# A 1-core adaLN, window-attention and token-MLP kernel: w1's first half paced, the zero fill of V in quarters, one small op with two inputs, masks in two steps, and a new order of the engines

## The chip, the cores and the metric

One Trainium2 chip, one of its cores. The metric is the time of one launch in microseconds (us) on the device, as a median of several runs.

Short names: PE is the matmul engine, PEld its weight loads, DVE the vector engine, ACT the scalar engine, POOL the GpSimd engine, SP the engine that hands over the DMA transfers. PSUM is the memory that matmuls write, SBUF the one that holds the other tiles. A hole is a stretch in which PE stands idle. The name before `<-` in a profile line is the tile that is written: `xn` is the normalised x and `nm` minus its mean, `kb` and `KT` are keys, `QT` queries, `VT` values, `psa` and `psb` scores, `et` their exps. A cast is a copy into another type. L193 and the like is the line of a helper that records every operation.

## The reference, cut to what matters

```python
# x: (1, 2048, 512), 32 heads of 16, window W = 256, F = 1792; weights in bf16
mod = (silu(c) @ w_mod)                     # six vectors of 512: sa, ca, ga, sb, cb, gb
h = layernorm(x) * (1 + ca) + sa
q, k, v = split(h @ wqkv)                   # per head
p = softmax(where(0 <= i - j < W, q @ k.T / 4, -1e9))
x = x + ga * ((p @ v) @ wo)
h = layernorm(x) * (1 + cb) + sb
u = gelu(einsum("bsd,sf->bdf", layernorm(h), w1) + b1)   # MLP over the 2048 tokens
x = x + gb * (einsum("bdf,fs->bds", u, w2) + b2).T
```

The attention is cut into 75 chunks of keys by queries. Each chunk is scores on PE, two exps on ACT (one of 128x1536 from `psa`, one of 128x512 from `psb`), a mask, then probabilities times V on PE. The first MLP matmul (`pu<-hb,w1p`) runs between the chunks as soon as rows of h are there. The rest of the MLP comes behind the last chunk.

## The kernel before

The whole program is a list of some 1,360 small operations. A fixed string of their numbers, `ORDER`, says in which order they are emitted. A letter behind a number (D, A, P) picks the engine. Each engine is given its own instructions in this order, so what is emitted behind a waiting instruction comes late too (PE's wait of 1.76 us in the prediction's lines).

```python
ORDER = """47 3 0 4 34 1 51 2 38 7 ... 1359 1360"""

VT = [kvpool.tile([P, 8, DH, 2 * DH], BF, name=f"VT{r}") for r in range(3)]   # V, block diagonal
vt_zero = [op("vz", {"DVE": 1.7, "POOL": 4.3},
              lambda e, r=r: (ve if e == "DVE" else po).memset(VT[r][:], 0.0), ...) for r in range(3)]

def e_nm(e, a, b):                       # nm = -mean
    mv, _, nm = box[box_key]
    (ve if e == "DVE" else po).tensor_scalar(
        out=nm[:, a:b], in0=mv[:, a:b, 0], scalar1=-1.0, scalar2=0.0, op0=ALU.mult, op1=ALU.add)

def emit_masks():                        # one operation on POOL, ahead of all scores
    if ADDED:
        emit_edges()
    ...                                  # block masks (maskt)

def load_w1(pair, half):                 # 14 pieces of 512 KB: 7 pairs, 2 halves
    t = box["w1"].tile([P, 8, 2 * P], BF, name=f"w1p{pair}", tag=f"w1p{pair}")
    sp.dma_start(out=t[:], in_=w1_v[:, 8 * half : 8 * half + 8, 2 * P * pair : 2 * P * (pair + 1)])
    w1t[pair, half] = t

def partials():                          # all seven first halves as soon as the modulation's SBUF is free
    freed = op("w1free", {"SP": 0.0}, e_w1, deps=mod_ops + warm_ops + [o_fm, masks_built], ...)
    for pair in range(NF // 2):
        w1_ops[pair, 0] = op("w1", {"SP": 0.4}, lambda e, pair=pair: load_w1(pair, 0), deps=[freed], ...)
```

The softmax here doesn't subtract the row's maximum and nothing guards it: scores larger than these inputs give would overflow.

## Time and profile before

| | |
|---|---|
| median | 273.39 us (273.29 to 273.47, 3 runs) |
| span of the profiled run | 271.3 us |
| PE busy | 251.4 us, 93% |
| w1's seven first pieces handed over | 43.0 to 53.9 us |

### The profile page before, as it was taken

The numbers are of one execution on the slowest core, as the hardware profiler recorded it, in microseconds if no ns is written. First come the engines' busy times: TensorE is split into PE (matmuls) and PEld (weight loads), VectorE is DVE, ScalarE is ACT, GpSimd is POOL, SyncE is SP. The second block draws the span as 40 slices with busy tenths as digits, with TensorE's granted clock in tenths as the row PEclk, the third lists the DMA queues.
The fourth block names the chain that finished last, engine by engine and source line by source line (L and its number), as shares of the span: only waits on it lengthen the run. The fifth ranks groups of instructions, "written<-read, shape, count | busy, mean of one in ns | idle before, by whom it ended". The sixth has DMA issues, their size and how long they took to land.

```text
span 271.3 us, 10569 instructions
## 1 busy us (share of the span) xinstructions
PE 251.4 (93%) x4737; PEld 137.8 (51%) x4737; DVE 208.6 (77%) x442; ACT 184.8 (68%) x277; POOL 68.5 (25%) x131
## 2 busy tenths in 40 slices
PE   8989979699999999778999999999999999999993
PEld 2566647256665664454464554444544444444441
DVE  4688899569887688999967799999999751134685
ACT  3269969579998999999999999999632741000000
POOL 8994460135021844151102400140000000000000
PEclk9999999899999999999999999999999999999999
DMA  6998104950000000000020000086199800011121
GB/s 207 323 349 211 5 2 133 289 130 5 2 5 2 5 6 2 2 2 2 10 76 2 2 2 4 2 228 163 54 408 377 324 1 4 19 39 39 62 89 65
DMA packets 31445, 24.80 MB, mean 91 GB/s; under 512 B 6056, under 2 KB 29608, under 8 KB 31400
## 3 DMA queue, kind: packets, MB, share of 16 engines
q1 hardware_dynamic: 31392, 24.13, 29.5%
q8 instruction: 37, 0.61, 0.9%
q14 instruction: 8, 0.07, 0.1%
q10 hardware_dynamic: 8, 0.00, 0.0%
HBM read 22.03 MB, written 2.10 MB: 89 GB/s over the span
## 4 chain that ended last, share of the span: by engine, by line
PE 73%; ACT 11%; DVE 11%; issue 4%
PE pu L193 35%; PE pxy L193 12%; ACT et L193 10%; PE pq L193 8%; PE psa L193 8%; PE pa L193 4%; PE pv L193 3%; DVE st L193 2%; DVE xn L193 1%; ACT lz L193 1%; DVE VT L193 1%; PE pt L193 1%; DVE et L193 1%; DVE nm L193 1%; PE ps_b L193 1%
## 5 line engine op out<-in xcount | busy, mean ns | idle before, releaser
L193 ACT ACTIVATE et<-psa 128x1536 bf16<-128x1536 f32 x75 | 109.1, 1454 | 10.0 <-PE psb L193 7.3
L193 PE MATMUL pu<-hb,w1p 128*128 128x512 bf16 x224 | 53.0, 380 | 0.1
L193 PE MATMUL pu<-guT,w 128*128 128x512 bf16 x224 | 49.2, 379 | 0.0
L193 ACT ACTIVATE et<-psb 128x512 bf16<-128x512 f32 x75 | 44.6, 598 | 0.0
L193 POOL TENSOR_SCALAR KT<-kb,mask_par 128x512 bf16<-128x512 bf16 (+1 forms) x36 | 23.3, 655 | 63.2 <-DVE kb L193 63.2
L193 PE MATMUL pxy<-et,VT 128*32 128x192 bf16 (+3 forms) x960 | 37.4, 234 | 0.7 <-DVE OT L193 0.5
L193 PE MATMUL pq<-h1T,wqkv 128*128 128x512 bf16 (+1 forms) x160 | 35.8, 350 | 2.2 <-DVE kb L193 1.3
L193 PE MATMUL pxy<-et,ones_bd 128*32 128x192 bf16 (+3 forms) x960 | 37.5, 233 | 0.0
L193 PEld LDWEIGHTS <-w 128*128 128x128 bf16 x224 | 21.9, 98 | 26.4
L193 PE MATMUL psa<-QT,KT 32*128 32x192 bf16 (+3 forms) x720 | 30.0, 230 | 5.1 <-ACT et L193 4.4
L193 PEld LDWEIGHTS <-w1p 128*128 128x128 bf16 x224 | 20.3, 98 | 24.9 <-issue 1.9
L193 PE MATMUL psb<-QT,KT 32*128 32x192 bf16 (+3 forms) x240 | 29.4, 231 | 2.6 <-issue 2.5
L193 PEld LDWEIGHTS <-KT 32*128 32x128 bf16 x960 | 15.6, 92 | 29.2 <-issue 27.5
L193 DVE SCALAR_TENSOR_TENSOR o<-pu,b2FM,bc_gb 128x512 f32<-128x512 f32 x16 | 12.0, 748 | 23.0 <-PE pu L193 23.0
L193 PEld LDWEIGHTS <-VT 128*32 128x32 bf16 x960 | 23.5, 97 | 7.8 <-issue 6.2
L193 DVE TENSOR_TENSOR et<-et,maskt 128x512 bf16<-128x512 bf16 (+2 forms) x56 | 23.8, 461 | 1.5 <-ACT et L193 1.4
L193 DVE CAST VT<-pv 64x512 bf16<-64x512 f32 x31 | 21.1, 686 | 2.9 <-PE pv L193 2.6
L193 DVE BATCH_NORM_STATS2 st<-x 128x6 f32<-128x512 bf16 x32 | 21.9, 684 | 1.8 <-DMA x<-in_A_x_dram 1.7
L193 PEld LDWEIGHTS <-ones_bd 128*32 128x32 bf16 x960 | 23.0, 97 | 0.1
L193 PEld LDWEIGHTS <-wqkv 128*128 128x128 bf16 x160 | 13.4, 99 | 14.7 <-issue 5.3
L193 PE MATMUL pv<-wqkv,h1T 128*32 128x256 bf16 x512 | 17.8, 274 | 0.8 <-DVE h1T L193 0.6
L193 DVE CAST QT<-pq 128x512 bf16<-128x512 f32 (+1 forms) x19 | 12.7, 670 | 5.8 <-PE pq L193 5.7
(91 smaller groups left out, 347.1 us busy)
## 6 DMA issues: line engine op xcount, KB each, us to landing
w1p<-in_B_w_dram SPq DMA_DIRECT2D x14, 512.0 KB, 7.5
w<-in_B_w_dram SPq DMA_DIRECT2D x14, 512.0 KB, 8.8
wmod<-in_w_mod_dram SPq DMA_DIRECT2D x6, 512.0 KB, 6.6
x<-in_A_x_dram SPq DMA_DIRECT2D x16, 128.0 KB, 5.7
out_dram<-otile SPq DMA_DIRECT2D x16, 128.0 KB, 1.7
wqkv<-in_A_wqkv_dram SPq DMA_DIRECT2D x2, 384.0 KB, 6.1
wqkv<-in_A_wqkv_dram SPq DMA_DIRECT2D x1, 512.0 KB, 5.9
wod<-in_A_wo_dram SPq DMA_DIRECT2D x1, 512.0 KB, 9.3
```

The source lines that it names most:

```text
L193: ins = call(*args, **kwargs)
```

## The change

Five parts: (a) each of the three zero fills of V's tile is cut into four; (b) `nm` on DVE is written with both inputs in SBUF; (c) edges and block masks become two operations, and scores wait for the edges alone; (d) a two-element copy on POOL from the exp tile of every third chunk into the w1 tile holds its load back; (e) `ORDER` is made anew. The arithmetic is the same, and PE has the same 4737 matmuls.

```diff
-47 3 0 4 34 1 51 2 38 7 35 8 39 5 82 56 40 81 6 46 9 57 54 83 10 45 ...
+49 3 0 4 46 84D 1 51 83D 2 47 7 41 8 44 5 93 56 42 90 6 54 9 57 35 94 ...
 ... (the whole order)
     def emit_masks():
-        if ADDED:
-            emit_edges()
-        if len(ADDED) == NU:
-            return
 ...
-            (ve if e == "DVE" else po).tensor_scalar(
-                out=nm[:, a:b], in0=mv[:, a:b, 0], scalar1=-1.0, scalar2=0.0, op0=ALU.mult, op1=ALU.add)
+            if e == "DVE":
+                ve.scalar_tensor_tensor(
+                    out=nm[:, a:b], in0=mv[:, a:b, 0], scalar=-2.0, in1=mv[:, a:b, 0], op0=ALU.mult, op1=ALU.add)
+            else:
+                po.tensor_scalar(...)            # as before
 ...
-    vt_zero = [op("vz", {"DVE": 1.7, "POOL": 4.3}, lambda ...: (...).memset(VT[r][:], 0.0), ...)
+    vt_zero = [[op("vz", {"DVE": 0.45, "POOL": 0.95}, lambda ...: (...).memset(VT[r][:, 2 * n : 2 * n + 2, :, :], 0.0),
+                   ...) for n in range(4)] for r in range(3)]
 ...
+    def touch_w1(pair, chunk):
+        t = w1t[pair, 0] = box["w1"].tile([P, 8, 2 * P], BF, name=f"w1p{pair}", tag=f"w1p{pair}")
+        po.tensor_copy(out=t[:, 0, 0:2], in_=et_of[chunk][:, 3, 0:2])
 ...
-            w1_ops[pair, 0] = op("w1", ..., deps=[freed], pos=start_of(1) + 2.0, ...)
+            w1_ops[pair, 0] = op("w1", ..., deps=[touched[chunk]], pos=chunk + 0.5, ...)
 ...
-    masks_built = op("masks", {"POOL": 6.0}, lambda e: emit_masks(), pos=-9.0)
+    edges_built = op("edges", {"POOL": 7.6}, lambda e: emit_edges(), pos=-9.0)
+    masks_built = op("masks", {"POOL": 2.8}, lambda e: emit_masks(), pos=20.0, sh=True)
```

## The prediction

> **What bounds the kernel now.** I first read the busy table by stage, with each row a stretch of the span and, for each engine, busy time, its instruction count, then granted TensorE clock, DMA share and GB/s.
>
> ```profile
> 35.00:42.00 7.00, 5.24 (x136) 3.15 (x124) 6.89 (x10) 4.88 (x7) 3.62 (x3) 1.00 0.01 2
> 42.00:49.00 7.00, 6.86 (x265) 4.84 (x262) 6.84 (x17) 6.75 (x10) 1.64 (x2) 1.00 0.74 194
> 49.00:56.00 7.00, 4.59 (x51) 1.77 (x50) 3.43 (x8) 2.44 (x4) 0.00 (x0) 0.76 1.14 278
> 56.00:133.00 77.00, 69.90 (x2079) 44.26 (x2078) 65.83 (x144) 75.47 (x109) 27.69 (x37) 1.00 0.03 9
> 133.00:196.00 63.00, 62.65 (x1293) 32.37 (x1292) 55.46 (x128) 59.45 (x91) 9.72 (x12) 1.00 0.21 54
> 196.00:266.00 70.00, 70.00 (x326) 31.78 (x325) 41.19 (x71) 12.99 (x24) 0.00 (x0) 1.00 0.37 136
> ```
>
> The columns are PE, PEld, DVE, ACT, POOL. From 56 to 133 us ACT (the exps of the attention) is busy 98% and paces the chunks; from 133 us to the end PE has no hole (62.65 of 63, then 70.00 of 70). So nothing after 56 us looks loose, and what can be won lies before it: two stages where PE and ACT both stand still, 35 to 42 and 49 to 56 us. Since everything behind is full, each us that PE wins there should move the end by one us.
>
> Next the timeline of single instructions, to see who holds these holes open (start, duration, engine, then idle before and releaser):
>
> ```profile
> 12.19 3.51 POOL L193 MEMSET VT<- 128x4096 bf16 x1
> 34.17 3.51 POOL L193 MEMSET VT<- 128x4096 bf16 x1
> ```
>
> ```profile
> 13.53 2.19 DVE L193 TENSOR_SCALAR nm<-mv 128x2 f32<-128x2 f32 x1
> 34.38 3.44 DVE L193 TENSOR_SCALAR xn<-x,mv,rs 128x512 bf16<-128x512 bf16 x1
> 38.34 0.42 DVE L193 TENSOR_SCALAR xn<-x,mv,rs 128x512 bf16<-128x512 bf16 x1
> ```
>
> Both slow DVE instructions start inside a zero fill of VT on POOL and end just after it (12.19 + 3.51 = 15.70 against 13.53 + 2.19 = 15.72; 37.68 against 37.82). The same xn takes 0.42 us four us later. They are not long, they are locked out.
>
> ```profile
> 15.80 0.60 PE L193 MATMUL pq<-h1T,wqkv 128*128 128x256 bf16 x4 [1.34 <-DVE kb L193]
> 38.47 1.02 PE L193 MATMUL ps_b<-wmod,sT_rep 128*128 128x512 bf16 x4 [1.76 <-DVE bc_sb L193]
> 51.41 0.21 PE L193 MATMUL psb<-QT,KT 32*128 32x128 bf16 x1 [2.47 <-issue]
> 51.74 3.48 PE L193 MATMUL pq<-h1T,wqkv 128*128 128x512 bf16 x8
> ```
>
> PE then waits 1.34 and 1.76 us for PSUM that the late DVE should have emptied. The third hole has another nature: in the middle of a chunk's scores PE stops 2.47 us and no semaphore is named. It falls inside the burst of the first half of w1: seven transfers of 512 KB handed over from 43.00 us on, SP busy with it 10.93 us. And the eight matmuls behind the hole take 3.48 us.
>
> The chain of waits has the same pieces: 2.19 us of nm, 3.36 of xn, 2.47 of issue and 3.41 of pq.
>
> **What the Trainium skill says.** "SBUF — State Buffer", section "SBUF: two separate sides": DVE and GpSimd share a port pair as an exclusive lock held for the whole instruction; a DVE instruction in a 2-port mode contends always, one with two SBUF inputs only against a GpSimd instruction that reads SBUF. The trace agrees: tensor_scalar from SBUF was held 2.19 and 3.44 us, while OT and casts, whose source is PSUM, kept 0.4 to 0.7 us during the fill at 24.56 us. It also explains nm rewritten with two SBUF inputs: a zero fill reads nothing. "Runtime: NRT & Kernel Launch", section "Instruction fetch mechanics": instructions come in 16 KiB blocks (256 instructions) over DMA. In the trace PE's instruction queue moves such a block from 48.95 to 50.14 us, inside the hole. "DMA: Bandwidth & Descriptors", section "Queues, rings and completion order": one DMA engine takes its queues in turn, so a block shares the engines with weights; that the wait follows from it no run shows yet. "TensorE: Matmul & The Clock Gate", Part 1: after an idle window PE runs at half clock. Here the weight loads behind the hole start 0.43 us apart (52.14, 52.57, 52.99) and the granted clock of the stage is 0.76.
>
> **The change part by part.**
> (a) Zero fill. Three fills of 3.51 us on POOL become twelve quarters; the built order puts seven on POOL and five on DVE. A quarter on POOL: 3.51 / 4 = 0.88 us (estimate). On DVE: the zero tile of half the size took 0.27, so some 0.54 us (estimate). PE recovers 1.34 + 1.76 = 3.10 us, ACT its waits of 1.66 and 1.96. Given back: a DVE instruction can still meet a quarter, at most 0.88 us; I put two such meetings of half that length on the path, 0.9 us. The five DVE quarters are 2.7 us: two lie before x has landed, where DVE idles 1.65 us, the other three fill later DVE time, say 0.4 us on the path. Net 3.10 - 1.3 = 1.8 us.
> (b) nm with two inputs: free of the lock against fills, the same small size. It is part of the 1.34 above.
> (c) Masks in two steps. The edge part ends near 9.45 us, the block masks (0.31 + 0.83 + 1.57 us, ending at 12.13) come later. The first scores start at 13.38, behind matmuls that wait for wqkv until 12.40, so their dependence was not the limit: 0 by itself. But POOL is free 2.7 us earlier for the KT copies of the second chunk (15.88 in before): 0.7 us, a guess between 0 and 1.5.
> (d) w1. The burst goes. A hole of the same kind stands at 87.19 us, 0.63 us long, exactly 1024 matmuls later at a DMA share of 0.02: so 0.63 belongs to the instruction stream and 2.47 - 0.63 = 1.84 us to the burst. With a short hole the clock should not fall: eight matmuls take 1.83 us elsewhere in the chain against 3.41, 1.58 us. Together 3.42 us. The seven small copies that pace the loads are some 0.2 us each on a POOL that is busy 25%.
> (e) The order of all engines was made anew. PE has the same 4737 matmuls; a few casts move from DVE to ACT. I book 0.5 us gain for it.
> Sum: 1.8 + 0.7 + 3.4 + 0.5 = 6.4 us, 273.4 - 6.4 = **267.0 us**.
>
> **Rivals.**
> (1) ACT paces at once. The time that PE wins is not used if exps can't come earlier. Against it: in the same holes ACT waits 1.66 + 1.96 + 2.60 + 1.96 = 8.18 us. If PE found work in all of it, the gain would be 8.2 us: 265.2.
> (2) DVE becomes the bound. It is busy 6.89 and 6.84 of 7 us from 35 to 49 us. But 3 us of that is a locked-out xn. If the quarters and their meetings eat all of (a), what is left is about 3.4 us: 270.
> (3) The hole at the instruction block stays. It is at a fixed count of matmuls, and there the first w1 piece is just being loaded: one piece instead of seven queued. If one is enough, 1.84 + 1.58 us are not won: 270.4. Against it: the load of about one piece in the later stage and even the five pieces from 175 to 189 us pass with PE 7.00 of 7, though at half the instruction rate.
> (4) The burst moves. The queue on SP keeps its order, and the built order is pieces 0, 1, 6, 3, then piece 0's second half, 4, 2, 5. Piece 6 is released last, at the 36th chunk, and holds those behind it, so four transfers follow each other near the 50th chunk, where PE first uses them some six chunks later. That is far from one each three chunks, but like the five pieces that pass unseen today. I expect no stall over 0.6 us.
> (5) The pacing copy reads the exp tile, so a late POOL keeps an exp buffer and stops ACT; the one for chunk 26 stands directly before chunk 32, which needs that buffer. I give it up to 1 us, 1 in 5.
>
> **Range and chances.** All won and nothing given back is near 265; another us from the new order makes the low end 263.5. One of the two large terms failing makes 270 to 270.5, the high end. A gain over 2% needs less than 267.9, only 0.9 above my value, so faster 0.64, same 0.35, slower 0.01; slower would need a new wait of 12 us and I see no candidate.
>
> **What would show it.** (a) no DVE tensor_scalar over about 1.3 us and no POOL memset over 1 us; PE's waits of 1.34 and 1.76 gone or under 0.6. (d) no hole over 1 us without a semaphore near the 990th matmul, granted clock 1.00 in every stage between 7 and 266 us, DMA share near 0.2 to 0.3 instead of 1.14 there. (1) ACT still 97% or more in the middle, all of it 6 us earlier; PE full from some 127 us on. Wrong would be: the PE hole as long with a single piece in flight, DVE waits moved to other instructions, ACT waiting for a pacing copy, or PE holes after 133 us at the four late transfers.

## More of the kernel before

The busy line of the page (us, share of the span, instructions), and one stage, 12 to 56 us, that the prediction does not show. The columns are PE, PEld, DVE, ACT and POOL (busy us and instructions), granted clock, DMA share and GB/s:

```profile
PE 251.4 (93%) x4737; PEld 137.8 (51%) x4737; DVE 208.6 (77%) x442; ACT 184.8 (68%) x277; POOL 68.5 (25%) x131
12.00:56.00 44.00, 37.39 (x970) 24.37 (x970) 37.28 (x76) 33.47 (x50) 20.20 (x21) 0.96 0.67 175
```

PE at 93% looks like a kernel with nothing left. The second line says where the rest is: in these 44 us neither PE (37.39) nor ACT (33.47) is full, and DVE and POOL are not either. Each waits for another, so this is the stretch to look at. The prediction reads it in detail.

## The result, and the profile after

| | before | after | ratio (95% interval) |
|---|---|---|---|
| first comparison | 273.34 us (273.20 to 273.47, 4 runs) | 268.82 us (268.50 to 269.56, 4 runs) | 0.9839 (0.9818 to 0.9860) |
| again, in the last batch | 273.76 us (271.81 to 275.25, 11 runs) | 268.24 us (268.03 to 269.32, 6 runs) | 0.9802 (0.9766 to 0.9837) |

Ratios are the mean time of one kernel's fast runs over that of the other's of the same rounds, so not quite the ratio of the medians quoted. The change gains 4.5 us in the first comparison (1.6%) and 5.5 us in the second (2.0%). It sits at the line of 2%; the first comparison is the one that the prediction was about, and there it is within 2%.

The busy line, and the same stages as in the prediction, of the kernel after:

```profile
PE 249.1 (93%) x4737; PEld 136.2 (51%) x4737; DVE 205.0 (77%) x439; ACT 186.6 (70%) x281; POOL 70.4 (26%) x146
35.00:42.00 7.00, 6.79 (x178) 3.98 (x162) 5.92 (x14) 6.82 (x10) 0.00 (x0) 1.00 0.01 2
42.00:49.00 7.00, 7.00 (x258) 4.76 (x250) 5.50 (x11) 6.58 (x10) 2.32 (x4) 1.00 0.02 6
49.00:56.00 7.00, 6.85 (x190) 4.11 (x178) 6.25 (x13) 6.81 (x10) 1.93 (x3) 1.00 0.01 2
56.00:133.00 77.00, 69.39 (x1967) 42.35 (x1970) 65.55 (x140) 73.95 (x107) 36.70 (x50) 1.00 0.12 31
133.00:196.00 63.00, 62.40 (x1246) 31.36 (x1239) 55.45 (x127) 56.53 (x89) 5.79 (x8) 1.00 0.39 105
12.00:56.00 44.00, 42.83 (x1165) 28.74 (x1163) 37.12 (x84) 41.00 (x60) 18.95 (x40) 1.00 0.37 101
```

The two loose stages are closed: PE 5.24 to 6.79 of 7 us in 35 to 42, and 4.59 to 6.85 in 49 to 56, where the granted clock is back from 0.76 to 1.00. Over 12 to 56 us PE is busy 42.83 of 44 instead of 37.39, ACT 41.00 instead of 33.47. But ACT from 56 to 133 us is now *less* full than before, 73.95 instead of 75.47. That line is the first hint that something won in front is given back there.

The instructions that were locked out, and two of the new quarters on POOL, in the timeline of the kernel after:

```profile
12.51 0.95 POOL L193 MEMSET VT<- 128x1024 bf16 x1
29.04 0.95 POOL L193 MEMSET VT<- 128x1024 bf16 x1
13.67 0.41 DVE L193 TENSOR_SCALAR xn<-x,mv,rs 128x512 bf16<-128x512 bf16 x1 [0.96 <-ACT rs L193]
31.21 1.04 DVE L193 TENSOR_SCALAR xn<-x,mv,rs 128x512 bf16<-128x512 bf16 x3
```

No xn is held by a fill any more: 0.41 us for one, 1.04 for three, against 3.44 for one before.

The pacing of w1, on POOL (the first and the last of the seven small copies) and on SP (start, and how long from the first to the last issue of the group):

```profile
59.40 0.32 POOL L193 COPY w1p<-et 128x2 bf16<-128x2 bf16 x1 [0.32 <-ACT et L193]
100.80 0.19 POOL L193 COPY w1p<-et 128x2 bf16<-128x2 bf16 x1
59.74 6.69 SPq L193 DMA_DIRECT2D w1p<-in_B_w_dram  x2
101.02 34.42 SPq L193 DMA_DIRECT2D w1p<-in_B_w_dram  x6
133.00:140.00 7.00, 7.00 (x188) 3.73 (x180) 3.62 (x8) 6.97 (x11) 1.81 (x3) 1.00 1.16 291
```

The copies end at 100.80 us, but the loads do not follow one by one. SP has its pieces in an order in which the last-released one stands third, so it waits for it. Two loads start at 59.7 and 66.1 us, two more at 101.0 and 101.4, and four follow each other from 131 to 134 us. The last line shows that this second, smaller burst (DMA share 1.16) costs nothing: PE is busy 7.00 of 7.

**Where the 4.5 us come from, stage by stage.** The start of each chunk's first exp cuts the span into stages that are comparable between kernels. The lengths are worked out from the traces: differences between those starts, and the end of the last matmul.

| stage | before | after | difference |
|---|---|---|---|
| start to chunk 0 | 14.0 us | 15.7 us | +1.7 |
| chunk 0 to 10 | 28.1 | 24.5 | -3.6 |
| chunk 10 to 15 (w1's burst in before) | 15.9 | 12.3 | -3.6 |
| chunk 15 to 30 | 34.3 | 34.1 | -0.2 |
| chunk 30 to 50 | 43.7 | 45.2 | +1.5 |
| chunk 50 to 70 | 44.2 | 44.9 | +0.7 |
| chunk 70 to the last matmul | 86.8 | 85.7 | -1.1 |
| sum | 266.9 | 262.4 | -4.5 |

At chunk 30 the kernel after is 5.7 us ahead, near the 6.4 us that were predicted for the end. Then it loses 2.2 us in the middle.

### The profile page after: what moved, and what is told of

Its sections match the earlier page's. It is cut to its first block, busy times and chain, and to the rows that moved or that the text cites. A ratio compares the mean times of both kernels' runs of the same rounds, so it can differ in the third digit from the quotient of the medians.

```text
span 266.8 us, 10593 instructions
## 1 busy us (share of the span) xinstructions
PE 249.1 (93%) x4737; PEld 136.2 (51%) x4737; DVE 205.0 (77%) x439; ACT 186.6 (70%) x281; POOL 70.4 (26%) x146
## 4 chain that ended last, share of the span: by engine, by line
PE 69%; DVE 14%; ACT 7%; DMA 5%; SPq 2%; issue 2%; DVEq 0%; ACTq 0%
PE pu L193 33%; PE pxy L193 10%; PE pq L193 9%; PE psa L193 9%; ACT et L193 5%; PE pa L193 4%; PE pv L193 3%; DVE VT L193 3%; DMA w<-in_B_w_dram 3%; DVE et L193 2%; DMA x<-in_A_x_dram 2%; DVE st L193 2%; SPq L193 2%; PE ps_b L193 1%; DVE h1T L193 1%
## 5 line engine op out<-in xcount | busy, mean ns | idle before, releaser
L193 PE MATMUL pu<-hb,w1p 128*128 128x512 bf16 x224 | 54.6, 380 | 1.2 <-DVE part L193 0.5
L193 PE MATMUL pq<-h1T,wqkv 128*128 128x512 bf16 (+1 forms) x160 | 34.1, 338 | 2.5 <-DVE kb L193 1.1
L193 POOL TENSOR_SCALAR KT<-kb,mask_par 128x512 bf16<-128x512 bf16 (+1 forms) x36 | 24.1, 679 | 34.7 <-DVE kb L193 18.3
L193 DVE TENSOR_TENSOR et<-et,maskt 128x512 bf16<-128x512 bf16 (+2 forms) x56 | 24.9, 479 | 0.5 <-ACT et L193 0.4
L193 DVE CAST VT<-pv 64x512 bf16<-64x512 f32 x30 | 20.5, 686 | 3.0 <-PE pv L193 2.1
L193 DVE TENSOR_TENSOR OT<-pxy,lz 128x256 bf16<-128x256 f32 x32 | 13.3, 415 | 9.5 <-ACT lz L193 9.4
L193 POOL TENSOR_SCALAR xn<-x,nm,rs 128x512 bf16<-128x512 bf16 x13 | 10.8, 834 | 32.2 <-DVE nm L193 22.6
```

The costliest lines, as they stand in the source:

```text
L193: ins = call(*args, **kwargs)
```

## The experiments

Twelve runs were made, all correct; two of them (in 8) repeat a kernel. The kernel before ran beside each batch: 273.09 us (272.68 to 274.94, 7 runs) in the first, 273.64 (271.63 to 274.90, 7) in the second, 273.76 (271.81 to 275.25, 11) in the third. Its own spread is several us in these batches, so differences under 1 us are read with care (experiment 5 shows what the spread is). A ratio is turned into us below by multiplying its distance from 1 by 273.4.

The theory at the outset: the gain is the burst's hole with its half clock (part d) plus the lock (parts a, b), each worth what the prediction booked. The rivals: the lock is not ended by cutting the fill, or the new order is what gains.

### 1. Part (d) alone, in the old order

```diff
     def load_w1(pair, half):
         t = box["w1"].tile(...)
+        if half == 0:
+            po.tensor_copy(out=t[:, 0, 0:2], in_=et_of[box["last"]][:, 3, 0:2])   # last exp tile written
         sp.dma_start(...)
 # ORDER: the seven first pieces stand before the scores of chunk 19, 22, ... 37
```

> The kernel before, its order kept, with one part alone: the first half of w1 goes out one piece each three chunks, each piece behind a two-element copy of the newest exp tile on POOL. Theory P (the parts add, the new order costs what is missing): the stop of 2.47 us in the middle of a chunk's scores and the eight matmuls at half clock go, the clock is 1.00 from 42 to 56 us, 273.3 - 3.4 to 4.0 = 269.3 to 269.9 us. Rival Q (the wait moves: ACT or DVE takes over at once, so a part alone gives little): the stop goes but the time falls by under 1.5 us, 271.8 or more.

Measured: 269.97 us (269.72 to 270.17), ratio 0.9878 (0.9842 to 0.9914), so 3.3 us. Here the pieces do come one each three chunks, the first at 60.8 us, so none is in flight at the place of the old hole. The timeline of PE at the place where before had its hole of 2.47 us, and the stage:

```profile
49.09 0.21 PE L199 MATMUL psb<-QT,KT 32*128 32x128 bf16 x1 [0.24 <-issue]
49.38 1.98 PE L199 MATMUL pq<-h1T,wqkv 128*128 128x512 bf16 x8
49.00:56.00 7.00, 6.91 (x163) 3.85 (x165) 5.46 (x12) 6.18 (x10) 1.51 (x3) 1.00 0.02 5
```

It is the same matmul. The wait is 0.24 us instead of 2.47, and the eight matmuls behind it take 1.98 us instead of 3.48. The burst made both. The trace also says how. PE's next block of instructions (by the DMA records of the packed trace, in which PE's instruction queue moves 16 KB at a time) is moved at 46.71 us here, when 1894 of PE's instructions have started. In before it is moved at 48.95 us, when 1985 have. So the block came 91 instructions later, at the very moment when PE ran dry, and the hole ended 1.3 us after the block had landed. Part (d) is confirmed in mechanism and in size (predicted 3.4).

### 2. The same burst, later

As in 1, but all seven pieces stand before the scores of chunk 19.

> The kernel before with the whole burst of seven w1 pieces kept together but moved some 17 us later, to about 60 us. If any instruction block of PE that is fetched in a burst comes late enough to stop PE: a stop of 2 to 3.5 us without a semaphore near matmul 1374 or 1502, time 272.5 to 273.5, as before. If the place in the chunk decides (late block, but PE waits for ACT there anyway, as in the changed kernel with the burst put back): the fetches come 2 to 3 us late but no stop is over 1 us, 270.0 to 271.5 us.

Measured: 271.91 us (271.73 to 272.69), ratio 0.9945 (0.9895 to 0.9994). The old hole is gone and two new ones stand under the later burst:

```profile
68.31 0.23 PE L199 MATMUL psa<-edge_n,edge_w 32*128 32x128 bf16 x2 [1.31 <-issue]
73.96 0.29 PE L199 MATMUL pxy<-et,ones_bd 128*32 128x256 bf16 x3 [1.57 <-issue]
63.00:70.00 7.00, 5.47 (x135) 3.34 (x135) 4.74 (x11) 5.38 (x7) 0.41 (x1) 1.00 1.19 298
```

The holes begin 127 recorded matmuls apart, and 512 and 640 weight loads behind the hole of the kernel before. A block of 256 PE instructions (37 blocks for the 4737 matmuls and as many weight loads in before) holds 128 pairs of weight load and matmul, so they stand exactly four and five blocks on. So the burst delays the block loads in both places where it was put, and what it costs depends on the place. In every profiled run each hole of over 0.5 us without a semaphore, from 7 us on, ended 1.2 to 1.6 us after a block had landed, the short ones far from any load too. Here the clock stays at 1.00 and about half of the gain is kept.

### 3. The burst in the new order

The kernel after, with part (d) taken out: the copies do nothing and all seven loads stand right behind the release of their SBUF.

```diff
     def touch_w1(pair, chunk):
-        t = w1t[pair, 0] = box["w1"].tile(...)
-        po.tensor_copy(out=t[:, 0, 0:2], in_=et_of[chunk][:, 3, 0:2])
+        pass
 # and deps=[freed] for the loads, which stand behind "w1free" in ORDER
```

> The changed kernel with one part undone: no pacing copies, all seven first-half pieces of w1 handed over as soon as their place is free, near chunk 18. Theory P: a stop of 1.5 to 3 us without a semaphore returns near the 990th matmul with half clock behind it, 268.8 + 3.4 to 4.0 = 272.2 to 272.8 us. Rival Q: the time rises by under 1.5 us. If the stop is at another place than the 990th matmul, the fixed count of matmuls is not what picks it.

Measured: 269.99 us (269.44 to 271.00), ratio 0.9884 (0.9842 to 0.9926). That is 1.2 us over the kernel after of the first comparison and 1.8 over its repetition in 8 (other batches both), not over 3. The stage of the burst and PE's only long wait in it:

```profile
56.00:63.00 7.00, 6.16 (x171) 3.46 (x169) 5.18 (x11) 5.73 (x11) 4.42 (x6) 1.00 1.20 300
62.13 0.29 PE L199 MATMUL psa<-QT,KT 32*128 32x256 bf16 x3 [0.83 <-ACT et L199]
```

PE's block of instructions is late here as well (59.39 instead of 56.42 us), but it arrives before PE needs it, so no long hole without a semaphore stands there, and the clock stays 1.00. In the new order the SBUF of the modulation comes free some 10 us later, so the burst falls on another place. **The same edit is worth 3.3 us in one order and some 1.2 to 1.8 in the other**; the parts do not simply add.

### 4. Cutting the fill, without changing the order

```diff
-   ... (ve if e == "DVE" else po).memset(VT[r][:], 0.0)
+   ... [(ve if e == "DVE" else po).memset(VT[r][:, 2 * n : 2 * n + 2, :, :], 0.0) for n in range(4)]   # one after the other
```

> The kernel before with one part alone: each whole zero fill of VT on POOL becomes four quarters at the same place, one behind the other; nm stays a tensor_scalar. Theory P: no DVE tensor_scalar is held longer than one quarter, so nm falls from 2.19 to at most 1.0 us and xn from 3.44 to at most 1.3 us, PE's waits of 1.34 and 1.76 us shrink to under 0.6 us each, 273.3 - 2.0 to 2.8 = 270.5 to 271.3 us. Rival L (the lock passes from quarter to quarter, POOL's next quarter gets it again before the waiting DVE instruction): nm and xn stay over 2 us and the time stays 273.3.

Measured: 275.12 us (three runs 275.0 to 275.3, one 272.7), ratio 1.0039 (0.9975 to 1.0103). POOL's fill and the xn beside it:

```profile
33.58 3.62 POOL L193 MEMSET VT<- 128x1024 bf16 x4
33.80 3.55 DVE L193 TENSOR_SCALAR xn<-x,mv,rs 128x512 bf16<-128x512 bf16 x1
```

The xn starts in the first quarter (33.80 against 33.58) and ends after the fourth (37.35 against 37.20). It could not get in at any of the three seams. nm fared better, 0.68 us instead of 2.19, in one place: it got in behind the quarter that it met. So cutting alone is no cure, and the theory that a meeting costs at most one quarter fell for xn. The three runs at 275 us are not the cut's doing: their mean clocks are 0.984 to 0.987, and the profiled one has the burst's hole at 3.51 us with half clock behind it for 6.8 us, where before has 3.4. Experiment 5 shows runs of the kernel before at the same clocks and times.

### 5. Moving the fill, without cutting it

The fill that meets xn (`79P`) takes the place of the harmless one (`80P`), which stands some ten chunks later than the moved one did, where no tensor_scalar meets it.

> The kernel before with one thing changed in its order: the fill of VT that met xn at 34 us takes the place of the harmless one at 24.6 us, and the third fill moves to where POOL is idle, near 48 us. Fills stay whole, w1 stays a burst, nm stays as it was. Lock theory: xn takes 0.40 to 0.45 us instead of 3.44, PE's wait of 1.76 us ahead of ps_b is gone, ACT's of 1.96 too; 273.1 - 1.5 to 2.0 = 271.1 to 271.6 us if the hole in the burst keeps its size (it has varied from 2.5 to 3.5 us, which makes 272.6 the top). Rival (another wait of that stage takes over, DVE being busy 6.9 of 7 us): xn is short but the time falls by under 0.7 us.

Measured: 270.36 us (270.27 to 272.06), ratio 0.9903 (0.9838 to 0.9968), so 2.7 us at first sight.

```profile
34.37 0.44 DVE L198 TENSOR_SCALAR xn<-x,mv,rs 128x512 bf16<-128x512 bf16 x1
49.60 0.21 PE L198 MATMUL psb<-QT,KT 32*128 32x128 bf16 x1 [2.61 <-issue]
```

The xn takes 0.44 us and PE's wait of 1.76 us behind it is gone. By the exps, 1.9 us are won at chunk 10, ahead of the burst (40.2 against 42.1 us). The burst's hole is still there, 2.61 us. But in this execution the clock behind it stayed at 1.00, while in the profiled execution of the kernel before it fell. That is luck and not the fill's doing, as the mean clocks of the single runs show:

| runs, by mean clock | kernel before (25 runs of three batches) | fill moved (4 runs) |
|---|---|---|
| 0.996 to 0.998 | 271.63, 271.81, 272.68 us | 270.27, 270.30, 270.41 us |
| 0.990 to 0.994 | 16 runs, 272.8 to 274.6 us | 272.06 us |
| 0.985 to 0.986 | 6 runs, 274.2 to 275.3 us | none |

Like against like, the moved fill wins about 1.3 to 1.5 us: 270.3 against some 271.7 us with the clock kept, 272.1 against some 273.4 (the usual run) with the clock lost. The clock records of the packed traces say what the three rows are. The profiled kernel before (0.991) has one stretch at half clock, 51.56 to 54.97 us, so 3.41 us long; experiment 4's (0.987) has one of 6.83 us, the moved fill's (0.996) none. One such stretch lowers the mean clock of a run by 3.41 x 0.5 / 271 = 0.006, which is the step between the rows. So, as an estimate for the runs without a profile, the rows have none, one and two stretches, and the times say what they cost: some 1.7 us in the usual run of the kernel before, nothing in three of 25, and 2.5 to 3.5 us in six. The hole's own length may differ along with it.

### 6. All small repairs in the old order: cut and not moved, or moved and not cut

The first has part (d) as in 1, the back-to-back quarters of 4, and the new nm. The second has part (d), the new nm, and whole fills moved as in 5.

> The kernel before, its order of instructions kept, with paced w1, the fills in quarters and nm with two inputs together; no new order, masks still in one step. Theory P: the parts add, 273.3 - 3.7 - 2.6 = about 267.0 us (266.3 to 267.8), 1 to 2.5 us faster than the changed kernel, whose new order gives that back. Rival Q (an ACT or DVE limit behind swallows it, in any order): 268.5 to 269.5 us, as the changed kernel.

> The order of the kernel before with three repairs: w1 paced, nm with two inputs, and the fills placed where no DVE instruction from SBUF meets them (whole, not split). If the parts add: 270.0 - 1.5 to 2.0 for xn and 0 to 1 for nm = 267.2 to 268.5 us, at or below the changed kernel's 268.8. If the locks were hidden behind ACT anyway: 269.5 to 270.0, as with w1 alone.

Measured: 269.70 us (269.29 to 269.88), ratio 0.9867 (0.9830 to 0.9903), for the first: xn is held 3.53 us as in 4, and it is only 0.3 us better than part (d) alone. The second: 267.66 us (267.40 to 268.20), ratio 0.9786 (0.9738 to 0.9834), so 5.9 us. Its stages (the lines are of its repetition in 8):

```profile
35.00:42.00 7.00, 6.89 (x198) 4.47 (x196) 5.81 (x16) 6.68 (x10) 0.00 (x0) 1.00 0.02 5
49.00:56.00 7.00, 6.65 (x212) 4.13 (x206) 5.54 (x13) 6.59 (x10) 2.49 (x4) 1.00 0.01 2
```

PE is as full as in the kernel after, without a new order, without quarters and without split masks. Its four runs lie within 0.8 us and all have a mean clock of 0.997 or more: with the hole, the half clock and its spread are gone too. By the exps it is 2.6 us ahead at chunk 10 (39.5 against 42.1 us: moved fill and new nm; 2.3 in its repetition), and part (d) alone gave 3.3, together 5.6 to 5.9, near the 5.9 measured. So the repairs add as far as this can tell. The new nm is shown at work: it stands inside a whole fill of 3.51 us that begins at 12.13 us, and is not held:

```profile
13.12 0.16 DVE L199 SCALAR_TENSOR_TENSOR nm<-mv 128x2 f32<-128x2 f32 x1
```

One hole without a semaphore is left in the repaired old order, at the block's edge where before has 0.63 us: 0.80 us here and 1.12 us in the repetition. There the block came from 78.70 to 79.89 us, between two paced pieces (one landed at 78.3 us, the next was handed over at 80.4), so no piece explains it. The kernel after has no such hole over 0.5 us.

### 7. Whole fills in the new order

The kernel after, with each tile filled by one whole memset on POOL at the place of its first quarter.

> The changed kernel with its fills whole again, 3.5 us each on POOL at the place of one of the quarters, in its new order. If cutting the fills is what ended the waits: a DVE instruction from SBUF is held over 2 us again, 268.8 + 1.5 to 3 = 270.3 to 271.8 us. Rival, from the fills in quarters on the old order, where the lock passed from quarter to quarter: it was the place in the order that ended them, no DVE instruction is held over 1 us, and the time moves by under 0.8 us except for KT copies that come later on POOL.

Measured: 272.34 us (271.88 to 273.34), ratio 0.9960 (0.9908 to 1.0012): 3.5 us over the kernel after of the first comparison.

```profile
31.31 3.51 POOL L193 MEMSET VT<- 128x4096 bf16 x1
33.32 2.94 DVE L193 TENSOR_SCALAR xn<-x,mv,rs 128x512 bf16<-128x512 bf16 x3
```

The lock is back (2.94 us for the three xn that take 1.04 in the kernel after), and POOL's copies of K come late behind the long fills. So cutting does matter in the new order, where the quarters lie apart with other work between them. How much of the 3.5 us is the lock and how much the longer work of POOL was not separated: PE waits 1.95 us for the copies of K and 1.57 us for DVE's `QT`. In the kernel after no tensor_scalar from SBUF meets a quarter at all, so what ends the lock there is distance between fill and tensor_scalar; cutting is one way to have the room for it.

### 8. Is the new order itself worth something, and is its late start its loss?

The kernel after once more as the yardstick, the second kernel of 6 beside it, and the kernel after with one word of the order moved: the first chunk's exp ahead of the two casts of K.

> The changed kernel itself, unaltered, as the yardstick of this batch. Both theories: 268.8 us (268.5 to 269.6 before), first exp at 15.7 us.

> The kernel before in its old order with three repairs (w1 paced, nm with two inputs, the two fills moved whole), run once more beside the changed kernel. Theory O (the new order as a whole costs what it starts later, some 1.2 us): 267.7 us, about 1.1 us under the changed kernel of the same batch, intervals apart. Rival N (the 1.2 us was noise between batches): within 0.4 us of the changed kernel.

> The changed kernel with one word of the order moved: the first chunk's exp goes on ACT ahead of the two casts of K that now stand before it. Theory O1 (the late first exp, 15.7 against 14.0 us, is what the new order loses): the first exp starts at about 14 us, all later chunks come about 1 us sooner, 267.8 us. Rival O2 (ACT's head start is used up by the casts that now come later and hold the keys of the second chunk): the first exp is early, the sixth chunk is where it was (27.3 us) and the time stays at 268.8.

Measured: 268.24 us (268.03 to 269.32) for the kernel after, 267.71 (267.44 to 268.24) for the old order with three repairs, ratios 0.9802 (0.9766 to 0.9837) and 0.9777 (0.9739 to 0.9816). The intervals overlap, but both hold the same noise of the kernel before. Set directly against each other, the six runs of each in this batch lie 0.66 us apart in the mean, with a 95% interval of about 0.1 to 1.2 us (worked out from the runs). So the new order gains nothing over the repaired old one, and it probably loses some tenths to 1.2 us. The stage table for the repaired old order: 13.9, 26.0, 11.8, 34.8, 43.8, 44.2 and 87.3 us. It has its gain in the same two stages, and from chunk 30 to 70 it takes 87.9 us as the kernel before does, where the kernel after takes 90.1. ACT's waits of these chunks in the kernel after (in total, times, longest) have one kind that neither of the other two has:

```profile
ACT et L193 <- PE psb L193: 1.6, 3, 1.0
```

The exp moved ahead gave 269.23 us (268.34 to 270.48), ratio 0.9829 (0.9790 to 0.9868): 1.0 us worse, part of which is the clock. Four of its six runs have a mean clock of 0.993, the yardstick's six 0.996 or more; the two with the clock kept took 268.3 and 268.6 us. The profiled run is the slowest, with half clock from 108.1 to 111.6 us. ACT first in the kernel after, then in the experiment, with PE's wait behind it:

```profile
14.90 0.82 ACT L193 ACTIVATE kb<-pq 128x256 bf16<-128x256 f32 x2 [1.05 <-PE pq L193]
15.62 1.44 ACT L193 ACTIVATE et<-psa 128x1536 bf16<-128x1536 f32 x1
```

```profile
14.20 1.45 ACT L199 ACTIVATE et<-psa 128x1536 bf16<-128x1536 f32 x1 [0.53 <-PE psa L199]
15.55 0.65 ACT L199 ACTIVATE kb<-pq 128x256 bf16<-128x256 f32 x2
15.98 0.38 PE L199 MATMUL pt<-identity,xn 128*128 128x128 bf16 x4 [0.85 <-ACT kb L199]
```

The exp does start 1.4 us earlier, but the casts now come later, PE waits 0.85 us for the PSUM that they empty, and the sixth chunk starts at 27.9 us instead of 27.2. So the late first exp is not the new order's loss; the casts in front of it earn it back. That theory fell: no run shows a gain from the earlier exp.

### 9. Part (c) alone

The repaired old order, with the block masks as their own operation behind the keys of the fourth chunk.

> The kernel before with the three repairs, and the edge and block masks built as two steps (part c alone on top): the block masks come on POOL after the keys of the fourth chunk instead of ahead of everything. Prediction's booking: 0.7 us gain (0 to 1.5) over the kernel without the split in this batch, so 267.0, because POOL's first copies of K start up to 2.7 us sooner. Rival Z (the keys wait for PE and ACT and not for POOL): POOL's first copies of K start where they did, within 0.3 us, and the time stays within 0.3 us of 267.7, or a little over it where the later masks on POOL delay a copy.

Measured: 267.69 us (266.89 to 268.67), ratio 0.9774 (0.9737 to 0.9812), against 267.71 without. POOL's first copies of K in the repaired old order, then with the masks split:

```profile
15.74 0.94 POOL L199 TENSOR_SCALAR KT<-kb,mask_par 128x256 bf16<-128x256 bf16 x2
```

```profile
14.90 0.94 POOL L199 TENSOR_SCALAR KT<-kb,mask_par 128x256 bf16<-128x256 bf16 x2 [2.01 <-DVE kb L199]
```

POOL was free 2.75 us earlier, but its copies start only 0.84 us earlier, because it then waits 2.01 us for `kb` from DVE. The lead at chunk 5 is 0.4 us (27.2 against 27.6) and at chunk 15 it is gone (51.7 against 51.6). Part (c) is worth nothing here.

## Why the prediction was right or wrong

The time, 268.82 us, lies in the range and 1.8 us over the value of 267.0: 4.5 us of the 6.4 that were forecast. A gain of over 2% was called the likelier outcome (0.64), and did not come in the first comparison (1.6%); the second lies at the line. By the prediction's own terms:

- **(d), 3.42 us: right in the old order, where it was reasoned.** It measured 3.3 us (experiment 1), with hole and half clock both gone. Two things were not in the step. The half clock is not the burst's fixed price: it is absent in one profiled run, 3.41 us long in another and 6.83 in a third (experiment 5). And in the new order the burst would have cost only some 1.2 to 1.8 us (experiment 3).
- **(a) with (b), net 1.8 us: the size near, the mechanism of giving back wrong.** The step said that a DVE instruction that meets a quarter waits at most for that quarter. Experiment 4 shows one that waited through all four. The built order avoids the meeting instead, so the 0.9 us booked for meetings were not paid: no tensor_scalar is held by a fill in the kernel after. In the old order the moved fill is worth some 1.4 us, and with the new nm 2.3 to 2.6 us stand at chunk 10. That two SBUF inputs free nm of a fill was right (0.16 us inside one, against 2.19).
- **(c), 0.7 us: wrong.** Experiment 9 measures 0.0. The failing step was "POOL is free 2.7 us earlier for the KT copies": it was, but the copies wait for DVE's cast.
- **(e), 0.5 us gain: wrong in sign, as far as it can be told.** Beside the repaired old order the new one is 0.5 us slower by the medians of one batch (0.1 to 1.2 by the interval) and 1.2 us across batches. Terms (a) and (d) together were booked at 5.2 us; the old order with only these repairs gains 5.9. What is missing to the 6.4 is therefore not a repair that failed, but (c) and (e), 1.2 us booked and nothing or less obtained.
- **"Each us that PE wins there should move the end by one us": holds for the old order and fails for the new.** The repaired old order is 5.8 us ahead at chunk 30, 5.8 at chunk 70 and 5.3 at the last matmul (261.7 against 266.9 us). The kernel after has 5.7 us at chunk 30 and 3.5 at chunk 70. In chunks 30 to 70 the trace shows ACT idle 3.1 us instead of 1.4 in the kernel before, while ACT as a whole has 186.6 us of work instead of 184.8. The stage is 2.3 us longer, of which 1.7 are ACT's idle time, and 0.6 is a copy of `part` that the new order gives to ACT at 175.7 us. The idle time is the step that failed: ACT's exps wait 1.6 us for PE's `psb` (experiment 8). Which words of the order do it was not taken apart; that stays open.
- **Rivals (1) and (2).** ACT does pace the middle, but at 96% (73.95 of 77 us from 56 to 133) instead of the 97% or more that were to show it. DVE did not become the bound: 5.92 and 5.50 of 7 us from 35 to 49.
- **Rival (4), the burst moves: came as described** (two, two, then four pieces together), and cost nothing, as expected. Rival (3), one piece is enough to make the hole, was not met at its place: the first piece comes at 60.8 us in experiment 1 and at 59.7 in the kernel after, when the block of the hole has long come. But where a block does come beside one piece (60.25 and 66.21 us in the kernel after), no hole over 0.5 us follows. Rival (5), the pacing copies hold ACT, did not show: without the copies (experiment 3) the kernel was not faster.

So the value lies within the range because its two large terms, (a) and (d), were right in size in the old order, where they were reasoned, and the mis-sized terms are the two that rested on a guess, (c) and (e). For the kernel as it was built there is some luck in it: there undoing (d) costs 1.2 to 1.8 us instead of 3.4, and undoing the cut of the fills 3.5 instead of 1.8 (with POOL's longer work in it), two errors of opposite sign.

## What to carry to other kernels

A hole without a semaphore next to a burst of DMA is a reason to look at the engine's instruction blocks: pace the burst, and look whether the hole stands at a block's edge. If a DVE tensor_scalar from SBUF is locked out by a POOL fill, move the fill to where none meets it, or give a small instruction two SBUF inputs; cutting the fill up did not help with the pieces back to back (xn 3.55 us), and did where they lay apart and met none. Before a new order of everything is credited, apply the single repairs to the old one: here three small edits did at least as well as a re-made order, and a term that no view of the profile carries (here a freer POOL, and "the new order") should be booked at zero.

## What the Trainium skill lacked or had wrong

- "Runtime: NRT & Kernel Launch", section "Instruction fetch mechanics", calls the cost of crossing a block "mostly hidden". Under a burst of seven 512 KB loads it was not: PE stopped 2.47 us in the kernel before, 3.51 us in another run (experiment 4) and 1.31 and 1.57 us under the moved burst (experiment 2), each time until 1.3 to 1.4 us after a block had landed. The page does not say that other DMA traffic delays the blocks, nor where to place large loads for it.
- "SBUF — State Buffer", section "SBUF: two separate sides", gives the lock for a whole instruction. It does not say that a run of GpSimd instructions can keep it: one DVE xn was held 3.55 us over four fills of some 0.9 us each, while the shorter nm got in after 0.68 us. What decides between the two no run shows.
- "TensorE: Matmul & The Clock Gate", Part 1, gives an idle window of some 3.4 us, free-running, for the fall to half clock. Here the clock fell (mean 0.76 over 7 us) after a hole of 2.47 us and stayed at 1.00 after one of 2.61 us, so a hole shorter than the window can be enough. In another run it fell with no hole over 0.99 us near (experiment 8, 108.1 us). Each stretch at half clock was 3.41 us long, or 6.83 in experiment 4's run. That the phase of a free-running window decides would fit the page, but is argued and not shown. By the mean clocks, the kernel before has none, one or two such stretches from run to run (an estimate), which goes with most of its spread (experiment 5).
